# Query blocks aligned with key blocks, one tail block for two heads, and the decay bias added by VectorE's min-pass

## The chip, the core and the metric

The kernel runs on one core of a Trainium2 chip. The metric is device time in microseconds: median 670.79 us of three runs before the change (670.02 to 671.18). The core's engines are TensorE (PE in the profile; PEld is its weight load), VectorE (DVE), ScalarE (ACT), GpSimd (POOL) and SyncE (SP), which issues nearly all DMAs.

## The reference

Three blocks follow each other: causal attention with a cumulative decay bias, a gated spatial MLP with a layer norm and a residual, and a second one of the same kind without residual. B = 4, H = 8 heads, S = 576 positions, D = 64; model width 512, inner width 1024.

```python
scores = scale * q @ k.T                      # per batch and head, 576 x 576
cum = np.cumsum(np.maximum(s, 0.0), axis=-1)
bias = -(cum[:, :, :, None] - cum[:, :, None, :])
scores = np.where(causal, -1e9, scores + np.minimum(bias, 0.0))
attn = exp(scores - max) ; attn = attn / (sum + 1e-9)
x = (attn @ v) as [B, S, 512]
h = gelu(x @ w_in); u, v = halves of h; v = layer_norm(v) * g
x = x + (u * (w_sg @ v + b_sg)) @ w_out       # first MoE block
h = relu(x @ w_in2); ...                      # second, the same with its own weights
```

A row of the softmax does not change when a constant of the row is added, so only +cum of the key column has to be added to the scores.

## The kernel before

**Work and stages.** Two heads make a pair; 16 pairs run one after the other, four per batch. When the four pairs of a batch are done, its first MoE block can start, and is interleaved with the attention of the next batch; after the last pair come the rest of the first block and the second one. The float32 MoE products are made of three float32r matmuls each (high and low parts; lines 347 to 350, 425 to 427, 451 to 456, 471 to 473, 493 to 495).

**Order.** Every step (`plan.add`) has a place, a number on a time scale where a head is 1, and the steps it has to follow; `Plan.emit` takes the ready step of the lowest place. The tables `PAIR`, `HEAD`, `MOE`, `WEIGHT` and so on hold the places, `ENG` holds the engine (A, D, P) of each copy or small operation by phase. The scheduler of the tile framework then sets each engine's order.

**One pair.** `ldqk` loads queries and keys of both heads, `transposes` (T) turns them on PE with an identity (lines 621, 625), so that head 0 lies in partitions 0 to 63 and head 1 in 64 to 127. Query blocks are cut as 64, 128, 128, 128, 128 rows (`QB`), so that block i sees 64, 192, 320, 448 and 576 keys (`QN`). In `scores` each piece of a block (`PARTS`) is a float32 matmul per head over 64 partitions (line 660), and a second, float32r one (line 663) multiplies rows of ones by the rows of `bias` and adds the cumulative bias into the same PSUM bank. Line 668 is VectorE's min-pass: it adds the causal mask (bfloat16, `mask`), multiplies by -0.125, writes the result to SBUF and gives the row minimum; a second small instruction of that line reads the minimum out. Line 674 is ScalarE's exponential with the row sum.

`rows_of_bias` (K) loads four rows of 576 numbers, 9 KB, from `cum_d` into one of two `bias` buffers. `seg` transposes the weights in 15 blocks of 128 x 128 per head (line 737, `SEG`) and copies them from PSUM (`x0` to `x3`). `values` (V3) multiplies by the values in 12 matmuls per head (line 748, `USE`). `denominators` (R), `spread` (B) and `finish` (F1) divide: the sums are turned, written to `rec_d` in DRAM, read back broadcast, and multiplied in (line 754). All this draws on six PSUM banks (`psa`), the MoE on two (`psm`).

**Start.** `keep_busy` gives PE eleven dummy matmuls (line 145). `cumulate` makes the running sum `c8`, splits it in a high and a low part `ch`, and writes it to `cum_d`.

Of the kernel before, what the change touches and what calls it, by code (L numbers as in the profile page):

```python
# [9 lines left out]
F32 = mybir.dt.float32  # L10
# [20 lines left out]
PA, PM, XB, RAW, LOW, QKW = 6, 2, 3, 32, 0, 32  # L31

PAIR = {"ldqk": -7.15, "ldv": -7.77, "T": -0.93, "K": -10.12}
PAIR0 = {"ldqk": -3.69, "ldv": 1.93, "T": -27.82, "K": -1.85}
HEAD = {"S2": -3.76, "S4": -5.12, "R": -10.75, "B": -15.6, "X0": -0.48, "X1": 0.01, "X2": -6.24, "X3": 0.59,
        "V3": 0.77, "F1": -15.8}
HEAD0 = {"S2": -6.73, "S4": -4.13, "R": -2.05, "B": -8.21, "X0": -0.95, "X1": -7.32, "X2": -5.75, "X3": -0.43,
         "V3": -5.72, "F1": -7.2}

MOE = {"Va": (1.98, 2.55), "Vb": (-16.53, -3.57), "Vc": (-15.5, 25.31), "U": (3.84, 4.64), "ZY": (6.68, 5.45)}  # L40
WEIGHT = {"wv": (-0.99, 0.33), "wu": (6.32, 1.86), "sg": (2.65, 7.0), "wo": (-3.21, 6.28), "ahead": 3.45}
MOE2 = {"Va": (-18.47, 16.21), "Vb": (2.06, 8.91), "Vc": (-3.94, 3.37), "U": (4.67, 13.35), "ZY": (8.44, 23.03)}
WEIGHT2 = {"wv": (-0.12, 5.87), "wu": (10.83, 13.19), "sg": (10.11, 10.44), "wo": (3.64, 1.59), "ahead": 4.44}

MORE = {"t2": 15.57, "d2": 4.3, "sp": 3.41, "sp2": -1.39, "cut": 0.48, "xr": -24.01, "w0": 11, "cp": -3}


ENG = {"ra": "PPD.", "wlo": "DPPP", "wmin": "PPDP", "whi": "ADPD", "xhi": "PPAA", "xlo": "PDPP", "xdh": "...A",
       "xdl": "APAP", "vn": "...D", "vhi": "...A", "vlo": "...D", "ghi": "PDAP", "glo": "PDDP", "mu": "PDPP",
       "var": "PDPD", "rg": "...A", "tq": "AAD.", "tk": "DAA.", "tr": "DDD.", "vc": "PDD.", "vcl": "PPD.",  # L50
       "vdup": "PPP.", "x0": "DAD.", "x1": "ADD.", "x2": "AAA.", "x3": "DAD."}


def fl(ap):
    return ap.bitcast(F32)
# [35 lines left out]
def attention_two_moe_kernel(  # L91
# [65 lines left out]

    mask = const.tile([128, MW], BF16, name="mask")
    mask_f = mp.tile([128, 128], F32, tag="g", bufs=3, name="mask_f")
    nc.gpsimd.memset(mask, 0.0)  # L160
    nc.gpsimd.memset(mask_f, 0.0)
    nc.gpsimd.affine_select(out=mask_f, in_=mask_f, pattern=[[-1, 128]], compare_op=ALU.is_ge, fill=MASKED, base=0,
                            channel_multiplier=1)
    nc.gpsimd.tensor_copy(mask[:, MW - 128:], mask_f)
    cum_d = dr.tile([BH, 2, S], F32, name="cum_d")
# [383 lines left out]
    raw_v = [ap.tile([128, NB, 2, D], F32, name=f"raw_v{i}") for i in range(2)]  # L549
    for t in raw_v:  # L550
        nc.gpsimd.memset(t[64:128, NT], 0.0)
    pts, ptr = ([[place(f"{t}{j}_{i}", 128 * (i + 1), dt, pn * j + 64 * i * (i + 1)) for i in range(NB)] for j in range(3)]
                for t, dt in (("p", F32), ("r", F32R)))
    for p in pts:
        for i in range(NB):
            nc.gpsimd.memset(p[i][:, QN[i] if i else 0:], 0.0)
    raws = place("raw", rn, F32, 3 * pn), place("rawr", rn, F32R, 3 * pn)
    qk_d = [dr.tile([128, rn], F32, name=f"qk_d{n}") if 2 * n >= QKW else None for n in range(BH // 2)]
    mx = [ap.tile([128, NB], F32, name=f"mx{i}") for i in range(3)]
    sums = [ap.tile([128, 32], F32, name=f"sum{i}") for i in range(2)]  # L560
# [36 lines left out]
    def plan_pair(plan, n, st):  # L597
# [330 lines left out]
```

## Time and profile before

| | before |
|---|---|
| runs | 671.18, 670.79, 670.02 us (median 670.79) |
| span of the profiled execution | 667.5 us |
| PE busy | 645.1 us, 97% of the span |
| VectorE, ScalarE, GpSimd busy | 383.1, 327.6, 204.8 us |
| mean granted TensorE clock | 0.986 of full |

The span runs from the first to the last instruction of one profiled execution; the profile gives no separate time of that execution, so its span stands beside the runs' median, 3.3 us below it. Busy time is the union of an engine's instructions; matmul records overlap, so what a matmul costs is read from one start to the next.

### The profile page before, as it was taken

To read this page: it belongs to the slowest core of one execution; us is meant where nothing else is said; L and a number is where in the kernel's file an instruction comes from. 1 tells how busy PE (TensorE), PEld (TensorE's weight loads), DVE (VectorE), ACT (ScalarE), POOL (GpSimd) and SP (SyncE) were. 2 spreads that over 40 slices of the span, in tenths; PEclk is the share of its full clock that TensorE was granted. 3 is DMA by queue.
4 is the path that set the end of the run, shared out by engine and by line. 5 is a ranking of instruction groups with operands and counts; after the bars stand their busy time and mean duration, and the time that the engine had idled before them with its cause. 6 is when DMAs were issued, how large, how long until landed. Compare 5 with 4: busy or idle time off the path is not lost.

```text
span 667.5 us, 12894 instructions
## 1 busy us (share of the span) xinstructions
PE 645.1 (97%) x4733; PEld 564.8 (85%) x4733; DVE 383.1 (57%) x1109; ACT 327.6 (49%) x846; POOL 204.8 (31%) x332
## 2 busy tenths in 40 slices
PE   7988889999999999999999999999999999999997
PEld 4766767789988889988889999987998998998996
DVE  5898776565557787567784588557952322112110
ACT  3677668785135574435572356436532516414311
POOL 3232225531321100301110434544683246033032
PEclk8799899999999999999999999999999999999999
DMA  8378551232342312432312342364341000010011
GB/s 214 91 221 206 153 155 51 57 80 71 102 120 64 111 39 72 109 104 75 103 29 67 112 139 63 109 200 138 95 125 42 32 32 19 31 35 15 17 45 50
DMA packets 88024, 60.01 MB, mean 90 GB/s; under 512 B 65301, under 2 KB 73493, under 8 KB 87961
## 3 DMA queue, kind: packets, MB, share of 16 engines
q1 hardware_dynamic: 86760, 58.89, 31.5%
q8 instruction: 37, 0.61, 0.4%
q10 hardware_dynamic: 1200, 0.30, 0.2%
q14 instruction: 27, 0.21, 0.1%
HBM read 44.59 MB, written 14.57 MB: 89 GB/s over the span
## 4 chain that ended last, share of the span: by engine, by line
PE 81%; DVE 7%; DMA 6%; issue 2%; ACT 2%; SPq 1%; POOL 1%; DVEq 0%; POOLq 0%; ACTq 0%
PE pp L737 7%; PE s L660 7%; PE acc L748 6%; PE pm L347 3%; PE pm L425 3%; PE pm L348 3%; PE pm L427 3%; PE pm L426 2%; PE pm L451 2%; PE pb L453 2%; PE pb L452 2%; PE pb L451 2%; PE pm L453 2%; PE pm L452 2%; PE pb L427 2%
## 5 line engine op out<-in xcount | busy, mean ns | idle before, releaser
L674 ACT ACTIVATE p<-p,mx 128x576 f32<-128x576 f32 (+4 forms) x160 | 88.3, 553 | 31.8 <-DVE mx L668 31.2
L660 PE MATMUL s<-qk 64*128 64x288 f32 (+4 forms) x384 | 71.6, 427 | 3.7 <-ACT qk L179 1.3
L668 DVE CUSTOM_DVE_ANT_0 p<-s,mask 64x64 f32<-64x64 f32 (+4 forms) x160 | 61.5, 422 | 13.1 <-PE s L663 12.6
L737 PE MATMUL pp<-idf,p 128*128 128x128 f32 x480 | 64.5, 277 | 2.5 <-DVE mx L668 1.5
L737 PEld LDWEIGHTS pp<-idf,p 128*128 128x128 f32 x480 | 54.2, 141 | 7.1 <-issue 2.1
L457 DVE TENSOR_TENSOR u<-u,pb 128x320 f32<-128x320 f32 (+1 forms) x33 | 14.6, 454 | 73.2 <-PE pb L456 73.2
L663 PE MATMUL s<-bias,ones 64*128 64x288 f32 (+3 forms) x192 | 53.8, 488 | 0.0
L748 PE MATMUL acc<-pt,raw_v 128*64 128x64 f32 (+3 forms) x768 | 52.2, 287 | 0.2
L748 PEld LDWEIGHTS acc<-pt,raw_v 128*64 128x64 f32 x768 | 42.2, 140 | 11.1 <-issue 2.5
L301 POOL TENSOR_TENSOR xl<-x,xh 128x576 fp32r<-128x576 f32 x20 | 28.8, 1457 | 69.2 <-ACT xh L179 69.0
L179 POOL CAST g<-u 128x256 fp32r<-128x256 f32 (+1 forms) x40 | 17.2, 441 | 106.6 <-DVE u L457 77.8
L660 PEld LDWEIGHTS s<-qk 64*128 64x128 f32 (+1 forms) x384 | 34.7, 185 | 16.2 <-issue 5.8
L179 DVE COPY pt<-pp 128x512 f32<-128x512 f32 (+1 forms) x72 | 37.2, 530 | 12.4 <-PE pp L737 11.8
L179 ACT COPY pt<-pp 128x512 f32<-128x512 f32 (+2 forms) x56 | 28.7, 532 | 31.1 <-PE pp L737 31.1
L378 POOL TENSOR_TENSOR sm<-sm,half_pow 128x1 f32<-128x1 f32 (+1 forms) x38 | 25.7, 681 | 49.4 <-DVE sm L377 38.2
L452 PE MATMUL pb<-sgl,vh 128*128 128x320 f32 (+1 forms) x132 | 39.0, 296 | 0.0
L451 PE MATMUL pb<-sgh,vh 128*128 128x320 f32 (+1 forms) x132 | 38.9, 296 | 0.0
L451 PE MATMUL pm<-sgh,vh 128*128 128x256 f32 (+1 forms) x124 | 38.0, 307 | 0.7 <-DVE u L457 0.7
L452 PE MATMUL pm<-sgl,vh 128*128 128x256 f32 (+1 forms) x124 | 36.7, 296 | 0.0
L497 ACT COPY o<-pb 128x512 f32<-128x512 f32 x13 | 7.5, 589 | 57.1 <-PE pb L495 55.1
L425 PE MATMUL pm<-xh,inh 128*128 128x320 f32 (+1 forms) x112 | 35.4, 316 | 0.0
L374 POOL TENSOR_SCALAR sm<-sm 128x1 f32<-128x1 f32 (+1 forms) x33 | 7.9, 240 | 87.7 <-DVE g L297 73.5
(255 smaller groups left out, 1967.5 us busy)
## 6 DMA issues: line engine op xcount, KB each, us to landing
x<-rec_d SPq DMA_DIRECT2D x32, 144.0 KB
x_d<-x SPq DMA_DIRECT2D x16, 288.0 KB
x<-x_d SPq DMA_DIRECT2D x16, 288.0 KB
raw<-in_q_dram SPq DMA_DIRECT2D x32, 128.0 KB
stage<-in_moe_w_in_dram SPq DMA_DIRECT2D x8, 512.0 KB
raw_v<-in_v_dram SPq DMA_DIRECT2D x32, 128.0 KB
stage<-in_moe_w_in_dram SPq DMA_DIRECT2D x16, 256.0 KB
out_dram<-o SPq DMA_DIRECT2D x16, 256.0 KB
```

Source lines behind the costliest of these rows:

```text
L179: (e.copy if e is nc.scalar else e.tensor_copy)(out_, in_)
L301: engine("xlo", phase).tensor_tensor(xl[:, kk, :S], x, fl(xh[:, kk, :S]), ALU.subtract)
L425: nc.tensor.matmul(pu, W["inh"][:, kk, f], xh[:, kk, c], start=(kk == 0), stop=False)
L427: nc.tensor.matmul(pu, W["inl"][:, kk, f], xh[:, kk, c], start=False, stop=(kk == KD - 1))
L451: nc.tensor.matmul(pz, vh[sb][:, f], W["sgh"][:, sb, c], start=(sb == 0), stop=False)
L452: nc.tensor.matmul(pz, vh[sb][:, f], W["sgl"][:, sb, c], start=False, stop=False)
L660: nc.tensor.matmul(st[a, e][:m, c0:c0 + w], st["qk"][rows, 0, qc], st["qk"][rows, 1, kc], start=True, stop=False)
L663: nc.tensor.matmul(st[a, e][:m, c0:c0 + w], ones[rows, :m], bias[n % 2][rows, kc], start=False, stop=True)
L668: nc.vector.tensor_tensor_reduce(out=pts[g][i][:m, kc], in0=st[a, e][:m, c0:c0 + w], in1=mask[:m, d0:d0 + w], scale=-0.125, scalar=3e38 if ...
L674: nc.scalar.activation(p, p, AF.Exp, bias=mx[g][:m, i:i + 1], scale=-1.0, accum_out=sums[n % 2][:m, NB * e + i:NB * e + i + 1])
L737: nc.tensor.transpose(ps[:, w:w + 128].bitcast(like), pt[:, kb * 128:kb * 128 + 128], turned if qb == kb and kb else ident)
L748: nc.tensor.matmul(acc[a][D * e:D * e + D, a0:a0 + w], raw_v[m % 2][:, kb, e], pair["x", e, i][:, c0:c0 + w], start=j in (0, 1), stop=j in ...
```

## The change

- **Blocks.** Query blocks are rows 0 to 127, 128 to 255, 256 to 383 and 384 to 511, as the key blocks are; block i sees 128 (i + 1) keys. The last 64 queries of both heads become one block of 128 rows: `qtail` holds head 0's queries in partitions 0 to 63 and columns 0 to 63, head 1's in the other half, zeros elsewhere, and two matmuls of 288 key columns over all 128 partitions score both heads (`tail_scores`, S4).
- **Scores.** `bank` makes the other blocks: 512 columns, then 128 and 384 in one bank, then 256 (S2, S3). There is no bias matmul.
- **Bias.** `rows_of_bias` now loads the bias broadcast: `cb` holds it for 512 keys in all 128 partitions for both heads, `ct` holds head 0's 576 keys in partitions 0 to 63 and head 1's in the others; three DMAs. `masks` (M) lets GpSimd write the masked diagonal blocks beside them with five selects. The min-pass (`reduce`) takes the bias as its second input in place of the mask. Pair 0's bias is spread by four float32 matmuls (line 612, 614) from `c8` instead of DRAM. Pairs 1 and 3 use MoE buffers that are still free; from pair 4 on there is one tile `cb`, so that K of pair n follows S3 of pair n - 1.
- **Transposes and values.** Ten blocks per head and five for the tail (`tails`) instead of 15 per head; 7 value matmuls per head instead of 12, over the same 1600 columns per head. The transposed weights lie in two tiles per head.
- **Buffers.** Values and the tail's weights have one buffer (before, values had two).
- **Places and engines.** All tables of places have new numbers, and `ENG` moves some copies and MoE operations between ScalarE, VectorE and GpSimd. `keep_busy` has 12 matmuls instead of 11.

```diff
-PAIR = {"ldqk": -7.15, "ldv": -7.77, "T": -0.93, "K": -10.12}
+PAIR = {"ldqk": -4.84, "ldv": -15.84, "T": -0.93, "K": -8.08}
...
-        for e in range(2):
-            nc.sync.dma_start(out=fl(bias[0][D * e:D * e + D:32]), in_=fl(ch[e:e + 1]))
-        nc.sync.dma_start(out=cum_d, in_=fl(ch))
+        nc.sync.dma_start(out=cum_d, in_=c8)
...
+            copy("tr", phase, st["qk"][:, 1, cr], pr[:, 1])
+            for e in range(2):
+                rows = slice(D * e, D * e + D)
+                copy("ts", phase, qtail[rows, REM * e:REM * e + REM], pr[rows, 0])
...
+                for i in range(2):
+                    nc.tensor.matmul(ps[i], st0["sel"][:, i], st0["c8"][:, :512], start=True, stop=True)
+                for i in range(2):
+                    nc.tensor.matmul(ps[2 + i][:, :288], st0["sel"][:, 2], st0["c8"][:, 288 * i:288 * i + 288],
+                                     start=True, stop=True)
...
-                nc.sync.dma_start(out=fl(bias[n % 2][::32]), in_=cum_d[2 * n:2 * n + 2].rearrange("h i t -> (h i) t"))
+            rows = cum_d[2 * n:2 * n + 2]
+            nc.sync.dma_start(out=st["cb"][:, :, :512],
+                              in_=rows[:, :512].rearrange("(o h) t -> o h t", o=1).to_broadcast([128, 2, 512]))
+            for e in range(2):
+                nc.sync.dma_start(out=st["ct"][D * e:D * e + D], in_=rows[e:e + 1].to_broadcast([D, S]))
+
+        def masks():
+            cb, ct = st["cb"], st["ct"]
+            for e in range(2):
+                nc.gpsimd.affine_select(out=cb[:, e, 512:].rearrange("p (i c) -> p i c", i=NT - 1),
+                                        in_=cb[:, e, :384].rearrange("p (i c) -> p i c", i=NT - 1), pattern=[[0, NT - 1], [-1, 128]],
+                                        compare_op=ALU.is_ge, fill=MASKED, base=0, channel_multiplier=1)
...
-                for e in range(2):
-                    rows = slice(D * e, D * e + D)
-                    nc.tensor.matmul(st[a, e][:m, c0:c0 + w], ones[rows, :m], bias[n % 2][rows, kc], start=False, stop=True)
...
+        def reduce(out_, ps, bias, lowest, more):
+            nc.vector.tensor_tensor_reduce(out=out_, in0=ps, in1=bias, scale=-0.125,
+                                           scalar=lowest if more else 3e38, op0=ALU.add, op1=ALU.min, accum_out=lowest)
+
+        def bank(groups):
+            ps = [[psa.tile([128, 512], F32, tag="a", name="s") for e in range(2)] for _ in groups]
+            parts = [(j, c0, i, e) for j, group in enumerate(groups) for c0, i in group for e in range(2)]
+            for j, c0, i, e in parts:
+                rows = slice(D * e, D * e + D)
+                nc.tensor.matmul(ps[j][e][:, c0:c0 + 128 * i + 128], st["qk"][rows, 0, 128 * i:128 * i + 128],
+                                 st["qk"][rows, 1, :128 * i + 128], start=True, stop=True)
+            for j, c0, i, e in parts:
+                g, d, s_ = (2 * n + e) % 3, 512 + 128 * i, ps[j][e]
+                p, low, cb = pts[g][i], mx[g][:, i:i + 1], st["cb"][:, e]
+                if i == NT - 1:
+                    reduce(p, s_, cb[:, :512], low, False)
+                    continue
+                if i:
+                    reduce(p[:, :128 * i], s_[:, c0:c0 + 128 * i], cb[:, :128 * i], low, False)
+                reduce(p[:, 128 * i:], s_[:, c0 + 128 * i:c0 + 128 * i + 128], cb[:, d:d + 128], low, i)
...
+        def tail_scores():
+            ps = [psa.tile([128, 512], F32, tag="a", name="s") for i in range(2)]
+            low = ap.tile([128, 1], F32, tag="low", bufs=2, name="low")
+            for i in range(2):
+                c = slice(288 * i, 288 * i + 288)
+                nc.tensor.matmul(ps[i][:, :288], qtail, st["qk"][:, 1, c], start=True, stop=True)
+            for i in range(2):
+                c = slice(288 * i, 288 * i + 288)
+                reduce(ptail[:, c], ps[i][:, :288], st["ct"][:, c], low, i)
+            weights(NT, ptail, low)
...
+        plan.add(f"K{n}", t0 + where["K"], rows_of_bias, [f"S3.{n - 1 if n > 4 else n - 2}", f"K{n - 1}"])
+        plan.add(f"M{n}", t0 + where["K"] + MORE["mk"], masks, [f"K{n}"])
...
+    SEG = [[(0, 0), (1, 0), (1, 1)], [(2, 0), (2, 1), (2, 2)], [(3, 0), (3, 1), (3, 2), (3, 3)]]
+
+    USE = [(0, 0, 0, 256, 0, 0), (1, 0, 0, 320, 1, 0), (0, 0, 256, 128, 0, 128), (1, 1, 0, 320, 1, 0), (1, 2, 0, 320, 1, 0),
+           (1, 3, 128, 192, 1, 128), (0, 0, 384, 64, 1, 256)]
```

Three places show how the instructions move. At the start, PE has this order before (`pst` and `pr` are the transposes of pair 0's queries and keys, `s` its scores, `pp` transposed weights):

```order
L621 MATMUL pst<-idf,raw 128x128 x8
L625 MATMUL pr<-idf,raw 128x128
L660 MATMUL s_252<-qk 64x64
L660 MATMUL s_253<-qk 64x64
L660 MATMUL s_262<-qk 128x192
L660 MATMUL s_263<-qk 128x192
L660 MATMUL s_288<-qk 128x288
L660 MATMUL s_289<-qk 128x288
L663 MATMUL s_252<-bias_186,ones 64x64
L663 MATMUL s_262<-bias_186,ones 128x192
L663 MATMUL s_288<-bias_186,ones 128x288
```

and this one now:

```order
L612 MATMUL bc<-c_143,sel 128x512 x2
L614 MATMUL bc<-c_143,sel 128x288 x2
L595 MATMUL pst<-idf,raw 128x128 x8
L599 MATMUL pr<-idf,raw 128x128
L650 MATMUL s<-qk 128x512 x2
L650 MATMUL s<-qk 128x128 x2
L650 MATMUL s<-qk 128x384 x2
L650 MATMUL s<-qk 128x256 x2
L673 MATMUL s<-qk,qtail 128x288 x2
```

Four bias matmuls come first, and all score matmuls of pair 0 stand in ten rows; before, 24 score and bias matmuls did. In the mixed stage, PE's visit to a pair's scores begins like this before (`pm` is a MoE product):

```order
L427 MATMUL pm<-xh,inl 128x256
L660 MATMUL s_1811<-qk 64x64
L660 MATMUL s_1812<-qk 64x64
L663 MATMUL s_1811<-bias_187,ones 64x64
L663 MATMUL s_1812<-bias_187,ones 64x64
L660 MATMUL s_1821<-qk 128x192
L660 MATMUL s_1822<-qk 128x192
L663 MATMUL s_1821<-bias_187,ones 128x192
L663 MATMUL s_1822<-bias_187,ones 128x192
```

and now the four blocks of both heads, without the tail, stand together:

```order
L462 MATMUL pm<-g_1804,outh 128x256
L463 MATMUL pm<-g_1804,outl 128x256
L650 MATMUL s<-qk 128x512 x2
L650 MATMUL s<-qk 128x128 x2
L650 MATMUL s<-qk 128x384 x2
L650 MATMUL s<-qk 128x256 x2
L461 MATMUL pm<-g_1804,outh 128x256
```

No bias matmul is left between them, and over the whole order the stretches of score matmuls (with their bias matmuls) go from 32 to 22. SyncE issues one bias load of a pair before (`raw` are queries and keys, `rec_d` the denominators):

```order
L593 DMA raw<-in_k_dram 64x2x64
L326 DMA x_d_108<-x 128x576
L481 DMA xr<-x_d_107 128x320
L630 DMA bias_187<-cum_d 4x576
L684 DMA rec_d_182<-rt 4x32x32
```

and three now:

```order
L576 DMA raw<-in_k_dram 64x2x64
L622 DMA cb<-cum_d 128x2x512
L625 DMA cb<-cum_d 64x576 x2
L686 DMA rec_d_142<-rt 4x32x32
L692 DMA x<-rec_d_142 64x576 x2
```

The denominators of the pair before and their spread come behind them in the queue.

## Rows read from the trace of the kernel before

**Rows 1.** The page: busy time of each engine; granted clock in 40 slices.
```profile
PE 645.1 (97%) x4733; PEld 564.8 (85%) x4733; DVE 383.1 (57%) x1109; ACT 327.6 (49%) x846; POOL 204.8 (31%) x332
...
PEclk8799899999999999999999999999999999999999
```

**Rows 2.** Busy by stage: PE, PEld, DVE, ACT, POOL (xcount); PEclk; DMA; GB/s.
```profile
0.00:10.00 10.00, 6.05 (x20) 2.46 (x20) 6.41 (x16) 2.54 (x3) 4.86 (x31) 1.00 0.81 198
10.00:26.00 16.00, 15.96 (x71) 12.38 (x72) 9.69 (x35) 9.37 (x26) 3.34 (x5) 0.57 0.62 150
...
42.00:58.50 16.50, 14.74 (x135) 11.40 (x133) 16.26 (x52) 12.38 (x35) 6.43 (x8) 1.00 0.76 201
...
200.00:350.00 150.00, 150.00 (x1243) 130.07 (x1242) 108.83 (x346) 82.45 (x220) 18.94 (x28) 1.00 0.29 79
```

**Rows 3.** PE's timeline: start us, us, line, operation, out<-in, shapes.
```profile
209.22 0.33 PE L660 MATMUL s<-qk 64*64 64x64 f32 x4
...
210.79 0.50 PE L347 MATMUL pm<-inh,xh 128*128 128x512 f32 x1
...
213.72 1.02 PE L660 MATMUL s<-qk 64*128 64x448 f32 x4
...
214.78 0.70 PE L660 MATMUL s<-qk 64*128 64x320 f32 x4
...
215.47 0.65 PE L660 MATMUL s<-qk 64*128 64x288 f32 x4
...
216.17 0.42 PE L471 MATMUL pm<-g,outh 128*128 128x320 f32 x1
216.43 0.31 PE L472 MATMUL pm<-g,outh 128*128 128x320 f32 x1
216.58 0.31 PE L473 MATMUL pm<-g,outl 128*128 128x320 f32 x1
...
224.81 1.46 PE L748 MATMUL acc<-pt,raw_v 128*64 128x64 f32 x30
226.20 0.77 PE L737 MATMUL pp<-idf,p 128*128 128x128 f32 x5
...
228.56 2.12 PE L737 MATMUL pp<-idf,p 128*128 128x128 f32 x18
230.44 0.36 PE L425 MATMUL pm<-xh,inh 128*128 128x256 f32 x1
```

**Rows 4.** Score records of PE (L660) in 50 us of the mixed stage.
```profile
200.00:250.00 50.00, 7.67 (x48) 3.57 (x48) 1.00 0.27 73
```

**Rows 5.** Groups of VectorE, 0:100 us: shapes xcount | busy, mean ns | idle.
```profile
L206 DVE SCALAR_TENSOR_TENSOR stage<-stage 128x512 int32<-128x512 int32 x12 | 8.6, 714 | 0.1
...
L668 DVE CUSTOM_DVE_ANT_0 p<-s,mask 128x448 f32<-128x448 f32 x10 | 6.1, 616 | 1.0 <-PE s L663 0.8
...
L668 DVE DVE_READ_ACCUMULATOR2_ANT mx<- 128x1 f32 x50 | 4.0, 80 | 0.0
L668 DVE CUSTOM_DVE_ANT_0 p<-s,mask 128x192 f32<-128x192 f32 x10 | 3.3, 347 | 0.0
...
L179 DVE COPY qk<-pr 128x128 f32<-128x128 f32 x6 | 1.7, 279 | 0.0
```

**Rows 6.** PE's timeline at the start.
```profile
10.04 2.38 PE L660 MATMUL s<-qk 64*64 64x64 f32 x12 [0.77 <-DVE qk L179]
...
20.73 1.97 PE L621 MATMUL pst<-idf,raw 128*128 128x128 f32 x8
```

**Rows 7.** The chain that ended last, 0 to 110 us: start us, us, what.
```profile
38.00 5.08 DMA stage<-in_moe_w_in_dram
```

**Rows 8.** Groups of GpSimd, whole run: the 128-column select.
```profile
L162 POOL TENSOR_SCALAR_AFFINE_SELECT mask_f<-mask_f 128x128 f32<-128x128 f32 x1 | 0.3, 288 | 0.0
```

**Rows 9.** Timeline of all engines, 33 to 34 us.
```profile
33.11 0.62 POOL L204 TENSOR_SCALAR stage<-stage 128x512 f32<-128x512 f32 x1 [1.32 <-ACT stage L203]
...
33.21 1.06 DVE L206 SCALAR_TENSOR_TENSOR stage<-stage 128x512 int32<-128x512 int32 x1
```

More of the change, by code (lines that the diff above doesn't have):

```diff
@@ L41 @@
[L41 to L51, printed above, removed]
+PA, PM, XB = 6, 2, 3
@@ L156, in attention_two_moe_kernel @@
     g_b = const.tile([128, DF], F32, name="g_b")
[L158 to L165, printed above, removed]
+    cum_d = dr.tile([BH, S], F32, name="cum_d")
     sr = mp.tile([BH, S], F32, tag="vh", name="sr")
@@ L695, in plan_pair @@
-        plan.add(f"ldqk{n}", t0 + where["ldqk"], ldqk, [f"cp{n}", f"T{n - 1}"])
+        plan.add(f"ldqk{n}", t0 + where["ldqk"], ldqk, [f"T{n - 1}"])
         plan.add(f"ldv{n}", t0 + where["ldv"],
-                 lambda: load(raw_v[n % 2], v, b, j, raw_v[n % 2][0:REM, NT]), [f"V3.{n - 2}"])
-        plan.add(f"T{n}", t0 + where["T"], transposes, [f"ldqk{n}", f"S4.{n - 2}"])
-        plan.add(f"K{n}", t0 + where["K"], rows_of_bias, [f"S4.{n - 2}", f"K{n - 1}"])
-        plan.add(f"S2.{n}", t0 + head["S2"], lambda: [f(i) for i in range(NT) for f in (scores, move)],
-                 [f"T{n}", f"K{n}", f"S4.{n - 1}", f"X3.{2 * n - 2}", f"X3.{2 * n - 3}"])
@@ L740, in seg @@
-            st["x"][i] = pair["x", odd, i] = ap.tile([128, w], F32, tag=f"pt{odd}{i}", name="pt")
-            copy(f"x{i}", phase, st["x"][i], ps[:, :w])
+            p, x = pts[n % 3], pair["x"][odd]
+            for w, (qb, kb) in enumerate(SEG[i]):
+                nc.tensor.transpose(ps[:, w * 128:w * 128 + 128], p[qb][:, kb * 128:kb * 128 + 128], idf)
+            w = len(SEG[i])
+            if i:
+                copy(f"x{i}", phase, x[1][:, :w, 128 * i - 128:128 * i], ps[:, :w * 128].rearrange("p (k c) -> p k c", k=w))
+            else:
+                copy("x0", phase, x[0][:, :384], ps[:, :384])
@@ new lines, in tails @@
+        def tails():
+            ps = [psa.tile([128, 512], F32, tag="a", name="pp") for i in range(2)]
+            for w in range(NT):
+                nc.tensor.transpose(ps[0][:, w * 128:w * 128 + 128], ptail[:, w * 128:w * 128 + 128], idf)
+            nc.tensor.transpose(ps[1][:, :128], ptail[:, S - 128:], idf)
+            for e in range(2):
+                x = pair["x"][e]
+                copy("x3", 2 * e + min(phase, 1), x[1][:, :, 256:],
+                     ps[0].rearrange("p (k h c) -> p h k c", k=NT, h=2)[:, e])
+                copy("x4", 2 * e + min(phase, 1), x[0][:, 384:], ps[1][:, REM * e:REM * e + REM])
@@ L834, in attention_two_moe_kernel @@
     s14b = place("s14b", DF, F32R, pos + 8 * 128)
[L835 removed]
+    stg2 = w2p.tile([128, S + REM], F32, name="stg2")
+    rest["v"] = w2p.tile([128, DF], F32R, name="restv")
     nc.vector.tensor_scalar(s14b[64:128], g_b[64:128], 0.0, 1.0, ALU.mult, ALU.add)
```

203 lines of the change are left out of this document (86 added, 117 removed), and 4 rows, old and new, of the table SEG.

## The prediction

> **What bounds the kernel now.** I read four views, in this order. First the page's busy shares and its forty slices: TensorE is busy 97% of the span, and its granted clock is 90% or more of full in all slices but three of the first five [rows 1]. Then the busy time by stage, which splits the run in two. From 200 to 350 us, where attention and the first MoE layer are interleaved, PE is busy 150.00 of 150.00 us at full clock, VectorE only 108.83 and ScalarE 82.45: every PE microsecond saved there is a microsecond of the run. Before the first MoE matmul at 94.4 us it is otherwise. From 10 to 26 us PE is busy 15.96 of 16.00 us, at a granted clock of 0.57, and from 42 to 58.5 us it is VectorE that is full, 16.26 of 16.50 us [rows 2]. So the same saving counts in full in the mixed stage and hardly at all once VectorE sets the pace. Third, PE's timeline around one pair of heads in the mixed stage, which gives the price of each kind of matmul [rows 3]. Last, the groups by shape for VectorE, and single rows for the start, the DMA chain and GpSimd [rows 5 to 9].
>
> **Scores and bias.** A start here is compared with the next start on PE, because records overlap. One pair's scores and bias take 209.22 to 210.79 and 213.72 to 216.17, that is 1.57 + 2.45 = 4.02 us, in two visits [rows 3]. The 320-column piece runs from 214.78 to 215.47, 0.69 us for both heads: float32 scores (two records per matmul, the heads in the two halves of the rows) and one float32r bias matmul. A float32r matmul of 320 columns costs 0.15 us (216.43 to 216.58), which leaves 0.54 us for the scores, 1.69 ns per column [rows 3]. At 0.69 us per 320 columns, the pair's 1600 columns should take 3.45 us; the other 0.57 us goes to entering and leaving, 0.285 us per visit.
>
> The change drops the bias matmuls. Row blocks of 512, 384, 256 and 128 columns remain, 1280 x 1.69 = 2.16 us per pair. The tail of both heads becomes one full-height matmul of 2 x 288 columns. No row shows a float32 matmul of that form. If the halves now overlap perfectly, its price per column is the same, 2 x 288 x 1.69 = 0.97 us; if they run one after the other it would be half, 0.49 us; if filling the array doubled it, 1.95 us. I take 0.97, because the 320-column row fits halves that run together. The new order has 22 separate stretches of half-height matmuls where the old one had 32, 1.4 per pair, so 0.40 us of entering. New sum 2.16 + 0.97 + 0.40 = 3.53 us: **0.49 us saved per pair**, with ends 0.97 and -0.49.
>
> **Transposes and values.** Eighteen transposes run from 228.56 to 230.44 [rows 3], 0.104 us each. A pair needs 25 in place of 30: **0.52 us saved**. The value matmuls keep their 1600 columns per head but go from 24 to 14 per pair, 20 records fewer. The visit of 30 records from 224.81 to 226.20 [rows 3] gives 0.046 us per record, so 0.92 us is the most that could go if width did not matter; it does, and I take 0.
>
> Per pair that is 1.01 us. In steady flow a pair passes every 25 us (48 score records, two pairs of heads, in 50 us [rows 4]), and five of sixteen pairs are scored before the first MoE matmul. **Eleven pairs x 1.01 = 11.1 us** are saved where PE is full. What covers the rest is VectorE at 73% of that stage: two more min-passes per pair are added to it. By its shapes a pass costs 1.05 ns per column, from (616 - 347)/256, plus 145 ns and an 80 ns read [rows 5]. Columns fall from 3200 to 3136, so +0.45 - 0.07 = +0.38 us per pair. Replacing the bfloat16 mask with a float32 spread bias as second input is not shown; I take the same rate, at best nothing gained, at worst a pass that takes twice as long, 14 x 0.225 + 3136 x 0.00105 = 6.4 us more per pair, with which VectorE would just fill the 25 us period.
>
> **The first stage.** Pair 0's scores hold PE from 10.04 to 20.73 us, at the low clock [rows 2, 6]. At 1.2 GHz the new form needs about 2 x 3.53 = 7.1 us, 3.6 us less, and its five transposes fewer save 1.0 at that clock. Against that, spreading pair 0's bias by matmul adds 1600 full-height columns, 2.7 us at 2.4 GHz and 5.4 at 1.2, of which PE's 4 idle us in the first 10 [rows 2] can take most. Net some -3 us. What comes next is VectorE's full stretch, and there the change adds work: 0.38 us per pair for passes and about 0.35 for two 64-column copies (half the width of the 279 ns copy [rows 5], less one narrower copy), 5 x 0.4 = 2 us after the narrower copies of transposed blocks are set off. Net -1 us, between -7 (the low clock, 0.43 of 16 us, is avoided altogether) and +8 (below).
>
> **Loads and masks.** Per pair SyncE now issues three bias loads, some 800 KB, where it issued one of 9 KB, and GpSimd five mask selects. A 512 KB weight load stood 5.08 us on the chain [rows 7], so 800 KB take 5 to 8 us. A 128-column select takes 0.288 us [rows 8]; the 384-column ones lie between that and three times it, nearest to the 0.62 us of a 512-column GpSimd pass [rows 9], say 1.9 us per pair (1.45 to 2.9). From pair 5 on the bias tile is single: load and mask stand between the last min-pass of one pair and the first of the next. About half of the 25 us period lies between them, less 4 us of passes still queued, so 8 us against 5 + 1.9. I take it as just hidden, cost 0. Values and the tail tile lose their second buffer too; they are read once per pair, and the next load has most of a period. After the last pair nothing of weight changes; I set new places of MoE steps at 0, +-2 us.
>
> **Sum.** The profiled span is 667.5 us; the median is 670.8 us, so 3.3 us lie around it, taken as fixed. 667.5 - 11.1 - 1 = 655.4, and with 3.3 the time is **658.7 us**. By its bounds it runs from 647 (11 pairs at 1.01 + 0.48 us, and the low clock gone: -23) to 668 (the +8 of the first stage; the tail at double price gives the same).
>
> **Rivals.**
> - *The late bias tile (slower).* Where load and masks take 11 us (8 + 2.9) instead of the 8 that are free, VectorE, which works in order, stands 3 us in each of 11 pairs, and the MoE passes queued behind it hold PE. 33 us lost, 11 gained: 691 us; half of it, if PE has half of the time other work, 675. It decides from 9 us on, where 11 pairs x 1.1 us eat the gain. For it: the load is ten times what it was, and SyncE's queue has other waits ahead of it. Against: DMA engines are busy only 0.29 in that stage [rows 2].
> - *The load on the first stage.* DMA is at 0.62 to 0.81 there [rows 2]; four bias loads join in. If one of them stands on the chain, +8 us: 667.
> - *Masks against VectorE.* A two-input pass took 1.06 us at 33.21 where its group's mean is 0.71, while GpSimd worked from 33.11 to 33.73 [rows 5, 9]. If half of the 25 early selects hold such a pass for 0.4 us, +5 us: 664. The Trainium skill, SBUF — State Buffer, "Who interferes with whom", states that a VectorE instruction with two SBUF inputs and a GpSimd instruction that reads SBUF exclude each other for a whole instruction. By that rule the min-passes, with one input in PSUM, are spared, and this row agrees.
> - *No low clock.* PE gets work from 6 to 10 us and stays at 2.4 GHz: 6 us more than forecast, 652.
> - *It doesn't save what it says.* The tail at 1.95 us per pair costs 11 x 0.97 = 10.7 us and gives back the gain: 669.
>
> **Chances.** Forecast (653 to 663) 0.60; no low clock 0.13; first-stage load or masks 0.12; late bias tile 0.10; tail at double price 0.05. The measurement tells 0.2% (1.3 us) from no change. Faster: 0.60 + 0.13 + 0.11 = 0.84; same 0.04; slower 0.12. The range 647 to 668 leaves out the late tile and the edges.
>
> **What would show it.** In the changed profile PE should stay at 150 of 150 us in the mixed stage, a pair's scores should take 3.5 us and not 4, and transposes 0.104 us each with 400 in place of 480 (320 + 80). The 320- and 512-column groups should show 1.69 ns per column for both heads together, and the tail 0.49 us per matmul. I am wrong if VectorE's min-passes wait for GpSimd or for the bias load in the mixed stage, if PE has gaps there, or if the first MoE matmul comes later than 94.4 us.

## The result, and the profile after

| | before | after |
|---|---|---|
| runs beside each other | 670.98 us median (670.02 to 672.25, 4 runs) | 649.59 us (647.77 to 652.21, 4 runs) |
| ratio, 95% interval | | 0.9693 [0.9658, 0.9727] |
| profiled execution: span, own time | 667.5 us | 650.4 us, 652.21 us |
| PE busy | 645.1 us | 627.0 us |

The change saves 21 us, 3.1%. The forecast was 12 us and 658.7; the measured time lies in its range of 647 to 668, but outside the 653 to 663 that it thought likeliest. The direction and the main term were right. The rest below asks where the other 9 us came from.

The page of the changed kernel (busy time of each engine; granted clock in 40 slices) answers to [rows 1]:

```profile
PE 627.0 (96%) x4086; PEld 536.2 (82%) x4086; DVE 406.3 (62%) x1258; ACT 332.1 (51%) x861; POOL 217.1 (33%) x327
...
PEclk9789997999999999999999999999999999999999
```

PE lost 18 us of busy time, VectorE gained 23. The busy time by stage (as [rows 2], with one stage more at 68 us), first of the changed kernel, then that stage of the kernel before:

```profile
10.00:26.00 16.00, 11.28 (x61) 8.49 (x60) 14.51 (x51) 10.05 (x27) 9.55 (x16) 0.79 0.98 243
42.00:58.50 16.50, 11.80 (x73) 8.32 (x75) 16.36 (x54) 10.85 (x30) 4.24 (x6) 0.79 0.72 190
68.00:94.40 26.40, 24.00 (x163) 17.69 (x160) 23.43 (x72) 16.57 (x47) 14.83 (x19) 1.00 0.80 195
200.00:350.00 150.00, 150.00 (x1085) 128.50 (x1086) 113.28 (x404) 82.10 (x225) 36.87 (x59) 1.00 0.40 114
```

```profile
68.00:94.40 26.40, 22.68 (x221) 18.52 (x219) 19.13 (x59) 17.61 (x50) 7.13 (x12) 0.94 0.58 165
```

From 200 to 350 us nothing has changed in kind: PE 150.00 of 150.00, VectorE 113.28. So the mixed stage is still PE's, as forecast. From 10 to 68 us VectorE is now nearly full (14.51 of 16 us from 10 to 26, where it was 9.69). The last rows of both are what the prediction had not looked at: from 68 us to the first MoE matmul of the kernel before, VectorE was busy only 19.13 of 26.40 us.

PE's timeline around two pairs of heads in the mixed stage of the changed kernel (start us, us, line, operation, out<-in, shapes) answers to [rows 3]:

```profile
309.88 1.13 PE L673 MATMUL s<-qk,qtail 128*128 128x288 f32 x4
310.85 1.04 PE L595 MATMUL pst<-idf,raw 128*128 128x128 f32 x8
311.72 0.27 PE L599 MATMUL pr<-idf,raw 128*128 128x128 f32 x1
...
315.56 2.43 PE L650 MATMUL s<-qk 64*128 64x512 f32 x16
317.92 0.39 PE L415 MATMUL pm<-xh,inh 128*128 128x256 f32 x1
```

The tail takes 309.88 to 310.85, **0.97 us**, the price that was chosen between 0.49 and 1.95. All four row blocks of both heads, in one visit, take 315.56 to 317.92 (2.36 us; the MoE matmul behind them starts there). The sum is 3.33, where 4.02 stood and 3.53 was forecast. Some pairs are scored in two visits of one head each, 1.92 + 1.49 us, so the mean over eleven pairs is higher: 3.7 (from all visits of these pairs, start to next start, in a second profile of the same kernel; 4.14 before). The eight transposes from 310.85 to 311.72 cost 0.109 us each; a pair has five fewer.

VectorE's groups by shape from 200 to 350 us (shapes xcount | busy us, mean ns | idle) show the min-pass with the spread bias:

```profile
L642 DVE CUSTOM_DVE_ANT_0 p<-s,cb 128x512 f32<-128x512 f32 x12 | 8.0, 685 | 1.2 <-PE s L650 1.1
...
L642 DVE CUSTOM_DVE_ANT_0 ptail<-s,cb 128x288 f32<-128x288 f32 x6 | 2.7, 450 | 0.0
```

685 ns for 512 columns is what the old pass would take (145 + 1.05 x 512 = 683), and 450 ns for 288 columns stand where the old pass took 445 in the same stretch: float32 and bfloat16 second inputs cost the same, as assumed. From 100 to 350 us one min-pass waits for GpSimd's masks, and none for the bias load (VectorE's waits: engine, output, line, what it waited for: us, times, longest):

```profile
DVE ptail L642 <- POOL cb L638: 1.1, 1, 1.1
```

Last, PE's timeline at the end of the first stage, before (with one row of the busy time by stage, whose 0.51 is the granted clock) and after:

```profile
67.40 0.66 PE L220 MATMUL pm<-idf,stage 128*128 128x128 f32 x4 [2.27 <-DMA stage<-in_moe_w_sg_dram]
...
68.10 4.64 PE L748 MATMUL acc<-pt,raw_v 128*64 128x320 f32 x48
...
68.00:70.00 2.00, 2.00 (x13) 1.14 (x13) 0.96 (x2) 1.97 (x7) 0.18 (x2) 0.51 0.36 66
...
94.37 0.47 PE L347 MATMUL pm<-inh,xh 128*128 128x512 f32 x1
```

```profile
61.55 0.66 PE L210 MATMUL pm<-idf,stage 128*128 128x128 f32 x4 [0.56 <-DMA stage<-in_moe_w_sg_dram]
...
80.95 0.50 PE L337 MATMUL pm<-inh,xh 128*128 128x512 f32 x1
```

In the kernel before, PE stood 2.27 us until 67.40 for a weight load, and its clock then fell (0.51 from 68 to 70 us). In the changed kernel the same matmuls wait 0.56 us, until 61.55, and the first MoE matmul comes at 80.95 instead of 94.37 us. It is tempting to take the wait and the clock for the cause, but two other profiles speak against it. The first two rows are the changed kernel again (run c0_after), the last two run f3_late below, whose pairs 0 to 4 and whose order are those of the kernel before:

```profile
64.26 0.65 PE L210 MATMUL pm<-idf,stage 128*128 128x128 f32 x4 [1.91 <-DMA stage<-in_moe_w_sg_dram]
...
83.19 0.50 PE L337 MATMUL pm<-inh,xh 128*128 128x512 f32 x1
```

```profile
68.00:94.40 26.40, 22.27 (x225) 18.27 (x226) 22.01 (x68) 19.70 (x55) 9.07 (x12) 0.99 0.61 173
...
93.86 0.66 PE L347 MATMUL pm<-inh,xh 128*128 128x512 f32 x1
```

With a wait of 1.91 us the changed kernel still starts its MoE at 83.19 us; with the clock at 0.99 from 68 to 94.4 us the old order still starts it at 93.86.

**An account.** I cut both profiles at 95 us, where both have scored pairs 0 to 4 in full. For each group of matmuls I add the time from each start to the next one, without idle gaps, times the granted clock. "Again" is the profile of run c0_after below, the same kernel.

| after 95 us | before | after | again | change |
|---|---|---|---|---|
| scores, bias, tail | 45.4 | 39.2 | 39.9 | -6.2, -5.5 |
| transposes | 44.1 | 37.3 | 38.8 | -6.8, -5.3 |
| values | 36.8 | 37.4 | 37.6 | +0.6, +0.8 |
| MoE | 435.1 | 427.8 | 428.3 | -7.3, -6.8 |
| PE idle | 3.6 | 1.5 | 2.8 | -2.1, -0.8 |
| lost to the low clock | 0.0 | 5.1 | 0.0 | +5.1, 0.0 |

Scores, transposes and values together give 12.4 and 10.0 us. But by 95 us the changed kernel has also scored pair 5's tail (0.97 us, at 89.67 and 92.13) and done eight query and key transposes (0.87 us) more than the old one, which is work moved forward and not work saved. Without it, and with six transposes of pair 4 that the second profile does only behind the cut, 10.6 and 8.8 us were saved (11.1 forecast). Of MoE's 7, 4.8 us had been done before the cut (5.6 against 0.8 us). So 6.6 us of later work lie ahead of 95 us: the early start. The other 2 to 2.5 us of MoE lie at the edge of the +-2 given for the new places; that the places made them cheaper is not shown.

Up to 95 us PE did about as much work in all: 72.4 us before (71.8 in f3_late), 72.9 and 71.0 after. Pairs 0 to 4 needed 6 to 7 us less of it, the four matmuls that spread the bias included; idle time rose from 13.1 to 16.2 and 17.6 us, and the low clock took 4.7 and 6.5 us instead of 8.5.

### The profile page after: what moved, and what is told of

The parts are those of the page before. It is cut to its first block, busy times and chain, and to the rows that moved or that the text cites. A ratio compares the mean times of both kernels' runs of the same rounds, so it can differ in the third digit from the quotient of the medians.

```text
span 650.4 us, 11947 instructions
## 1 busy us (share of the span) xinstructions
PE 627.0 (96%) x4086; PEld 536.2 (82%) x4086; DVE 406.3 (62%) x1258; ACT 332.1 (51%) x861; POOL 217.1 (33%) x327
## 4 chain that ended last, share of the span: by engine, by line
PE 78%; DVE 9%; DMA 7%; ACT 2%; issue 2%; POOL 1%; SPq 0%; ACTq 0%; DVEq 0%; POOLq 0%
PE acc L755 7%; PE s L650 5%; PE pp L726 5%; PE pm L337 3%; PE pm L338 3%; PE pm L415 3%; PE pm L340 3%; PE pm L416 2%; PE pm L417 2%; PE s L673 2%; PE pm L441 2%; PE pst L595 2%; PE pm L442 2%; PE pm L443 2%; PE pb L441 2%; PE pb L443 2%
## 5 line engine op out<-in xcount | busy, mean ns | idle before, releaser
L666 ACT ACTIVATE p<-p,mx 128x128 f32<-128x128 f32 (+3 forms) x128 | 70.8, 556 | 15.8 <-DVE mx L642 14.9
L169 ACT COPY pt<-pp 128x384 f32<-128x384 f32 (+2 forms) x92 | 41.6, 486 | 32.8 <-PE pp L726 30.2
L452 POOL TENSOR_TENSOR g<-u,g 128x256 fp32r<-128x256 f32 (+1 forms) x32 | 25.7, 808 | 93.0 <-ACT g L169 93.0
L169 ACT CAST g<-u 128x256 fp32r<-128x256 f32 (+1 forms) x48 | 20.5, 433 | 63.9 <-DVE u L447 61.0
L755 PE MATMUL acc<-pt,raw_v 128*64 128x320 f32 (+4 forms) x448 | 52.9, 373 | 0.1
L642 DVE CUSTOM_DVE_ANT_0 p<-s,cb 128x128 f32<-128x128 f32 (+2 forms) x128 | 48.3, 416 | 2.9 <-PE s L650 2.6
L650 PE MATMUL s<-qk 64*128 64x384 f32 (+3 forms) x256 | 47.3, 467 | 0.8 <-DVE qk L169 0.8
L631 POOL TENSOR_SCALAR_AFFINE_SELECT cb<-cb 128x384 f32<-128x384 f32 x32 | 17.1, 555 | 89.2 <-DMA cb<-cum_d 61.2
L726 PE MATMUL pp<-idf,p 128*128 128x128 f32 x320 | 45.4, 281 | 1.2 <-DVE x L761 1.2
L650 PEld LDWEIGHTS s<-qk 64*128 64x128 f32 x256 | 26.5, 194 | 15.4 <-issue 7.1
L415 PE MATMUL pm<-xh,inh 128*128 128x256 f32 (+1 forms) x112 | 35.1, 313 | 0.0
L337 PE MATMUL pm<-inh,xh 128*128 128x512 f32 x84 | 34.5, 410 | 0.6 <-DVE xh L169 0.6
```

Of the source, the lines that this page charges most:

```text
L169: (e.copy if e is nc.scalar else e.tensor_copy)(out_, in_)
L337: nc.tensor.matmul(ps, xh[:, kk, c], hi, start=(kk == 0), stop=False)
L415: nc.tensor.matmul(pu, W["inh"][:, kk, f], xh[:, kk, c], start=(kk == 0), stop=False)
L642: nc.vector.tensor_tensor_reduce(out=out_, in0=ps, in1=bias, scale=-0.125, scalar=lowest if more else 3e38, op0=ALU.add, op1=ALU.min, accu ...
L650: nc.tensor.matmul(ps[j][e][:, c0:c0 + 128 * i + 128], st["qk"][rows, 0, 128 * i:128 * i + 128], st["qk"][rows, 1, :128 * i + 128], start= ...
L666: nc.scalar.activation(p, p, AF.Exp, bias=low, scale=-1.0, accum_out=sums[n % 2][:, c:c + 1])
```

## Experiments

Twelve kernels. "Before" in each is the median beside it. Those named e and q let the scheduler order the instructions anew, which turned out to be a change of its own; the four named f hold the order of every engine. No run holds the order alone, without an edit.

**c0_after**: the changed kernel again. 

> The changed kernel again, unedited, beside the others of this group: 649.6 us as before, between 647 and 653. The span of each run says what lies outside it: 1.8 us if the four runs so far are typical, not the 3.3 that the prediction took.

Measured 651.44 us (649.08 to 652.52, before 669.76), ratio 0.9718 [0.9694, 0.9742]. In every run of both kernels the time is 1.7 to 1.9 us above the span. The 3.3 us of the prediction were these 1.8 and the difference between one execution and the median of others. Over both groups the gain is 18 to 21 us.

**e2_mixed, e1_early**: work added to PE (e1_early with `n < 5` as its condition).

```diff
-                nc.tensor.matmul(ps[j][e][:, c0:c0 + 128 * i + 128], ...)
+                for _ in range(2 if i >= 2 and 6 <= n < 11 else 1):
+                    nc.tensor.matmul(ps[j][e][:, c0:c0 + 128 * i + 128], ...)
```

> The same doubling in pairs 6 to 10 in place of pairs 0 to 4: the same 7.6 us of TensorE work, now where PE is busy 150 of 150 us. Theory of the prediction: +7.6 us (within 1.5). Rival (VectorE or the bias load sets the pace of a pair there): +0 to +3.

> The changed kernel, in which pairs 0 to 4 issue the score matmuls of their 384- and 512-column blocks twice (the second overwrites the first with the same numbers): 896 columns of both heads at 1.69 ns, 1.5 us of TensorE work per pair, 7.6 us in all, before the first MoE layer has really begun. Theory A, as the prediction had it (VectorE sets the pace until the first MoE matmul): the added work is hidden, 0 to +1 us. Theory B (TensorE sets the end there too, because VectorE is full only up to about 60 us): +2 to +4, the work of pairs 3 and 4. Theory C (every TensorE microsecond counts everywhere): +7.6.

Measured: e2_mixed 668.78 us, +17.3 on c0_after; e1_early 677.98, +26.5. Both above every theory, and the traces say why. In e2_mixed PE's work (as in the account, whole run) is 633.5 us against 618.2, +15.3, twice the estimate. In several of these pairs the two copies of one head now stand together. From e2_mixed's PE timeline:

```profile
225.09 1.98 PE L651 MATMUL s<-qk 64*128 64x512 f32 x4
227.00 0.39 PE L415 MATMUL pm<-xh,inh 128*128 128x256 f32 x1
```

Four records of one head take 1.91 us, 0.95 per block with entering and leaving (they start 0.43 us apart), while two heads in turn take 0.86 for the same block (run f1_early, below). One head alone costs as much as both. (The Trainium skill, TensorEngine Tiling (Array Packing), "Key Properties", lets tiles of the array work in parallel; here they do where the two heads' matmuls alternate.) So the 15.3 us of work cost 17.3 us of time, though in a new order (2.1 us more idle time, 1.9 less of low clock): in the mixed stage PE's work counts in full, as forecast. In e1_early the work grew by 13.4 and the idle time by 9.1 us. Its order differs in thousands of rows, and it decides nothing.

**q2_places**: the kernel before with the new places of the MoE steps and weights alone. 

> The kernel before, with nothing but the changed kernel's places of the MoE steps and weights (the tables MOE, WEIGHT, MOE2, WEIGHT2 and five entries of MORE). The prediction set the new places at 0, +-2 us: 669 to 673. Rival (the first MoE matmul at 81.0 us in place of 94.4 comes from the places): 661 to 666, with the first MoE matmul before 90 us.

Measured 681.36 us (before 669.76), 1.7% slower, first MoE matmul at 95.32 us. Alone in the old kernel the new places cost 11.6 us. Both theories fell, and how much of the 21 us they are worth in the new one can't be told by this.

**q3_nobias**: the kernel before without its bias matmuls. 

> The kernel before without its 192 float32r bias matmuls, all else kept (the decay bias is left out of the scores). By the prediction's row price, 1600 columns per pair at 0.15 us per 320, 0.75 us per pair: -8.3 us over eleven pairs, up to -12 if the early pairs count too. Rival (the bias matmuls cost what lies between their starts and the next starts in the trace, 12.6 us for six pairs in 200 to 350 us): -23 us and more. What the aligned blocks and the tail add or take is then the rest up to the changed kernel's -21.

Measured 667.88 us (before 669.72), ratio 0.9971 [0.9953, 0.9989]. PE's work fell from 636.5 to 625.3 us, 0.70 per pair, as the row price said; but its idle time rose from 16.7 to 23.7 us and the low clock took 11.5 us instead of 8.5. The work went, and the new order gave most of it back, as the next two runs bear out.

**f3_late, f3_early**: the same, with the order held. Each engine's instructions are chained in the order of the kernel before, and only the bias matmuls of some pairs go (their score matmuls then end the accumulation themselves). The cut shows f3_late; f3_early has `n < 5` in place of `n >= 5`.

```diff
-                    nc.tensor.matmul(st[a, e][:m, c0:c0 + w], ..., start=True, stop=False)
-                for e in range(2):
+                    nc.tensor.matmul(st[a, e][:m, c0:c0 + w], ..., start=True, stop=n >= 5)
...
+                for e in range(0 if n >= 5 else 2):
                     ...
                     nc.tensor.matmul(st[a, e][:m, c0:c0 + w], ones[rows, :m], bias[n % 2][rows, kc], start=False, stop=True)
```

> The kernel before without the bias matmuls of pairs 5 to 15 (their decay bias is left out of the scores), and with every engine's instructions held in the order that they had in the kernel before, so that nothing but these 132 matmuls goes. The first try without them let the scheduler find a new order: TensorE's work fell by 11.2 us (0.70 per pair), but its idle time rose by 7. If TensorE's work alone sets the end of the mixed stage and the order is what gave it back, eleven pairs at 0.70 to 0.75 us are seen in full: -7 to -9 us. Rival (another engine sets the pace when TensorE gets faster): 0 to -4.

> The same with the bias matmuls of pairs 0 to 4 left out in place of those of pairs 5 to 15, the order held again: 60 matmuls, 3.5 to 3.8 us of TensorE work at full clock (a little more where the clock is low). Theory A, as the prediction had it (VectorE sets the pace until the first MoE matmul, so this is hidden): 0 to -1 us. Theory B (VectorE sets it to about 60 us only, and then TensorE): -1 to -2.5. Theory C (it counts in full): -3.5 to -5.

Measured: f3_late 662.25 us (before 669.24), ratio 0.9905 [0.9868, 0.9942], -7.0 us. The visits of a pair's scores show where:

```profile
306.45 1.34 PE L660 MATMUL s<-qk 64*64 64x64 f32 x12
307.72 0.50 PE L347 MATMUL pm<-inh,xh 128*128 128x512 f32 x1
...
310.66 2.05 PE L660 MATMUL s<-qk 64*128 64x448 f32 x12
312.64 0.41 PE L471 MATMUL pm<-g,outh 128*128 128x320 f32 x1
```

1.27 and 1.98 us stand for 1.57 and 2.45 in [rows 3], 0.77 less; the mean over the eleven pairs is 4.14 to 3.42, 8 us in all. The time fell by 7.0 (interval 3.9 to 8.8). In the profile the time behind 95 us fell by 6.9: 8.5 us less of score work by the account, 1.1 us lost to the low clock and 0.7 more for values. So within the interval this saving counts in full in the mixed stage; the rival's 0 to 4 just touches it.

f3_early: 663.86 us, ratio 0.9919 [0.9891, 0.9947], -5.4 us (interval 3.5 to 7.3). Theory C by its size, but not by its place. VectorE's first min-pass, before and then here:

```profile
12.65 0.22 DVE L668 CUSTOM_DVE_ANT_0 p<-s,mask 64x64 f32<-64x64 f32 x1 [2.56 <-PE s L663]
```

```profile
9.81 0.22 DVE L670 CUSTOM_DVE_ANT_0 p<-s,mask 64x64 f32<-64x64 f32 x1 [0.56 <-PE s L660]
```

It comes 2.8 us earlier. The ends of the last min-pass of each pair, in us, one profile each (f3_late has pairs 0 to 4 as before, c0_after is the changed kernel again, so these two rows show the scatter):

| pair | 0 | 1 | 2 | 3 | 4 |
|---|---|---|---|---|---|
| before | 21.4 | 35.9 | 52.2 | 68.0 | 86.7 |
| f3_late | 21.0 | 36.7 | 52.9 | 69.8 | 85.8 |
| f3_early | 18.1 | 30.9 | 48.3 | 64.0 | 82.7 |
| after | 20.9 | 35.4 | 51.6 | 67.7 | 82.7 |
| c0_after | 21.5 | 36.4 | 53.3 | 69.9 | 85.2 |

The gain of f3_early is made at pairs 0 and 1, where in the kernel before PE runs at the low clock (0.57 from 10 to 26 us) and VectorE is busy 9.69 of 16 us. What pairs 2 to 4 save adds nothing: against "before" the lead stays at 4 us. By 95 us f3_early has done 5.2 us of MoE work, where the kernel before has done 0.8. The changed kernel, which spreads pair 0's bias first, has no such lead at pairs 0 to 3. Its 4.0 us at pair 4 stand in one profile; between c0_after and f3_late they are 0.6.

**f1_early**: PE work added to pairs 0 to 4 of the changed kernel, order held, heads in turn.

```diff
+                if n < 5 and i >= 2 and e == 1:
+                    for f in range(2):
+                        rows = slice(D * f, D * f + D)
+                        EXTRA.append(nc.tensor.matmul(
+                            ps[j][f][:, c0:c0 + 128 * i + 128], st["qk"][rows, 0, 128 * i:128 * i + 128],
+                            st["qk"][rows, 1, :128 * i + 128], start=True, stop=True).ins.name)
```

(`EXTRA` tells the held order which matmuls are new.)

> The changed kernel with the score matmuls of the 384- and 512-column blocks of pairs 0 to 4 issued twice, the two heads in turn so that their halves run together, and every engine's order held as in the changed kernel: 1.5 us of TensorE work per pair, 7.6 us in all. In the changed kernel VectorE is busy 23.4 of 26.4 us from 68 to 94.4 us, more than in the kernel before (19.1). Theory A (hidden by VectorE until the first MoE matmul): 0 to +2. Theory C (counts in full): +7 to +9. Between them: what counts is the part behind the score matmuls that VectorE waits for.

Measured 652.18 us (before 669.24), ratio 0.975 [0.9716, 0.9785], against 0.9718 of c0_after: +0.3%, 2 us, with intervals that overlap (the widest difference they allow is 6 us, below theory C's 7 to 9). The work is there and the start of the MoE lies between those of the two profiles without it (80.95 and 83.19 us):

```profile
11.54 1.05 PE L655 MATMUL s<-qk 64*128 64x512 f32 x4
12.40 1.06 PE L650 MATMUL s<-qk 64*128 64x128 f32 x8
...
81.16 0.50 PE L337 MATMUL pm<-inh,xh 128*128 128x512 f32 x1
```

The doubled 512-column blocks take 11.54 to 12.40 us, 0.86. PE's idle time is 15.7 us, where it was 17.7 and 20.4. In the changed kernel the early stage hides most of 7.6 us of added PE work (theory A). That VectorE sets its pace there is the likeliest reading (23.43 of 26.40 us busy), but no run made VectorE faster.

**e5_dma0**: pair 0's bias loaded instead of spread by matmuls (`if n == 0` made false). 

> The changed kernel with pair 0's bias loaded from DRAM like the others, without the four matmuls that spread it. If VectorE sets the pace of the first stage, its first min-pass (12.8 us) comes later by the write of the sums, the load of 800 KB and the masks, some 4 to 8 us, and most of it counts: +3 to +7 us. Rival (TensorE's 3.2 us at the start are what counts): -2 to 0.

Measured 676.31 us (before 669.72), +25 on c0_after. The first min-pass comes at 19.14 us, waiting for the load, against 13.7 in c0_after. That lies within the 4 to 8 us expected for it; the time missed the +3 to +7, and the order is another one, which starts the MoE at 125 us. The first part is shown, the size of its effect is not.

**e3_load, e4_mask**: the bias load, and the masks, three times from pair 5 on (`for _ in range(3 if n > 4 else 1)` around them). 

> The changed kernel with each bias load from pair 5 on issued three times, 2.4 MB in place of 0.8 MB per pair. In the changed kernel the masks of pairs 5 to 15 end 0.7 to 12.5 us before the next min-pass. If the single bias tile is just hidden, as forecast, 6 to 10 us more of load exceed that in most pairs: VectorE waits 2 to 8 us per pair, and about half of it reaches PE: +15 to +40 us. Rival (hidden with much room): 0 to +3.

> The changed kernel with the five mask selects of pairs 5 to 15 done three times: 1.9 us of GpSimd become 5.8, no DMA added. By the room read in the trace (0.7 to 12.5 us, under 3.9 in five of eleven pairs) VectorE waits some 9 us in all, and PE half of it at most: 0 to +5 us. If GpSimd's selects hold VectorE's passes as well (the shared port), the min-passes that lie beside them get longer by up to 4 us per pair: +10 us and more, and the group's mean of the 512-column min-pass rises above 0.70 us.

Measured: e3_load 698.49 us, +47 on c0_after, more than the +15 to +40 expected; its order is a new one. VectorE's waits from 100 to 350 us (columns as above):

```profile
DVE ptail L643 <- DMA cb<-cum_d: 34.3, 7, 6.9
```

There the slower rival happens: the first pass of a pair waits for its bias. In the changed kernel it is hidden. Its SyncE, GpSimd and VectorE around one pair:

```profile
321.04 0.37 SPq L622 DMA_DIRECT2D cb<-cum_d  x1
...
326.64 0.53 POOL L638 TENSOR_SCALAR_AFFINE_SELECT cb<-cb 64x64 f32<-64x64 f32 x2
...
330.08 0.45 DVE L642 CUSTOM_DVE_ANT_0 ptail<-s,cb 128x288 f32<-128x288 f32 x1
```

The load is issued at 321.04 us, the two last masks start at 326.64 and take 0.53, so all is there 6.1 us after the issue and 2.9 before the next min-pass. "Just hidden" was right (8 us free and 6.9 needed were forecast), and the room is small. e4_mask: 664.71 us, +13 where 0 to +5 was expected; VectorE's waits for masks are 5.6 us in five pairs, and order and masks can't be told apart. But its 512-column min-pass answers the question of the port:

```profile
L643 DVE CUSTOM_DVE_ANT_0 p<-s,cb 128x512 f32<-128x512 f32 x20 | 13.4, 687 | 0.7 <-PE s L651 0.6
```

687 ns beside three times the GpSimd selects, 685 without. The Trainium skill, SBUF — State Buffer, "Who interferes with whom", spares a pass with one input in PSUM, and this agrees.

**f4_warm**: dummy matmuls in two gaps of PE, order held (the first 32 here, 24 more behind pair 1's tail transposes).

```diff
+            if n == 0:
+                for _ in range(32):
+                    EXTRA.append(nc.tensor.matmul(ps[1][:, 384:384 + 128], qtail, idf, start=True, stop=True).ins.name)
```

> The changed kernel, order held, with dummy matmuls (idf by qtail, into unused columns) in two gaps of TensorE: 32 behind pair 0's tail scores, 24 behind pair 1's tail transposes, so that the granted clock does not fall behind these gaps (each low stretch of some 7 us loses 2.5 to 3.5 us of TensorE's work). If TensorE sets the end there, -3 to -6 us. If VectorE does, 0 to -2. If the clock falls all the same elsewhere: 0.

Measured 667.36 us, +16. It failed as a test. The dummies share a tile with the tail scores and so wait for VectorE's min-pass on it:

```profile
20.93 10.17 PE L680 MATMUL s<-idf,qtail 128*128 128x128 f32 x64 [3.31 <-DVE low L642]
30.93 1.04 PE L595 MATMUL pst<-idf,raw 128*128 128x128 f32 x8
```

They run from 20.93 to 30.93 us, pair 1's transposes start at 30.93 in place of 19.43, and the first MoE matmul comes at 98.72 us. It shows only that a delay of pair 1, 11.5 us here, reaches the start of the MoE and the end; the 24 later dummies add to it. What the low clock costs stays open.

## Why the prediction was right, and where it was off

The measured 649.6 us lie outside the 653 to 663 that got 0.60. By number they are nearest to the rival "no low clock" (652), which did not happen. So the main term was right by its mechanism, and that the time fell in the range owes something to the range's width.

- **Scores, 0.49 us per pair**: 0.41 to 0.48 by the account, pair 5's tail included. Nearly right, the tail's 0.97 to the digit. f3_late shows the price of the bias matmuls by itself, 0.77 in the pair shown.
- **Transposes 0.52, values 0**: 0.52 and 0.45 in the two profiles (five fewer per pair, at 0.105 and 0.107 us each, 0.104 before); values +0.06. Right.
- **Eleven pairs in full**: right. PE 150 of 150 us; added work costs its own time (e2_mixed), removed work gives it (f3_late).
- **The first stage, -1 us**: mis-sized, and this is the main miss. Its parts were off both ways: "net some -3 us" at pair 0 did not come (21.4 became 20.9 and 21.5), and pair 3 ends at 67.7 and 69.9 instead of 68.0 and, in f3_late, 69.8. The step that failed is "What comes next is VectorE's full stretch": the window from 42 to 58.5 us was taken for all that lies before the first MoE matmul, and what PE saves there was put at nothing. From 68 to 94.4 us VectorE was busy 72% of the time (83% in f3_late), and by 95 us 6.6 us of later work (4.8 of MoE, 1.8 of attention) were done. The 6 to 7 us that PE no longer spends on pairs 0 to 4 are of that size, and f3_early too moved 4.4 us of MoE ahead by removing PE work there. On the other side f1_early adds such work almost without cost. What lets the saved work through stays open: neither the weight load's wait nor the clock at 68 us explains it, by the two profiles above, and the new order, which puts 16 MoE matmuls among pair 3's value matmuls, was not tried by itself in the changed kernel.
- **Places, 0 +- 2**: MoE matmuls 2 to 2.5 us cheaper, idle time after 95 us 1 to 2 less. At the edge, if the places are their cause.
- **3.3 us outside the span**: 1.8. This did not move the forecast, which is the median of 670.8 less 12.1; the other 1.5 is the profiled execution's distance from that median.
- **Where the 9 us lie.** Five are in the profiles: the span fell by 17.1 and 16.8 us instead of 12.1. The early start gave 6.6 in place of 1, MoE and idle time 4.6 and 2.8 in place of 0, attention 0.5 and 2.3 less than forecast, and one of the two profiles lost 5.1 us to the low clock. The other four are scatter: the profiled execution was 1.5 us below its median before (667.5 + 1.8 against 670.8) and 2.6 above it after (652.2 against 649.6).

Rivals: the late bias tile did not happen, but e3_load shows that it is real, once 1.6 MB more are loaded per pair. An early bias load did stand on the chain that ended last in the changed kernel (start, us, what):

```profile
52.97 6.11 DMA cb<-cum_d
```

In c0_after it was 7.29 us, from 54.95. The forecast time of that rival, 667 us, did not come with it: pair 3 ended at 67.7 and 69.9 us, against 68.0 and 69.8 with the old loads. "Masks against VectorE" meant VectorE's early passes with two inputs, and these did get longer, the 12 of this group from 714 [rows 5] to 889 ns on average:

```profile
L196 DVE SCALAR_TENSOR_TENSOR stage<-stage 128x512 int32<-128x512 int32 x12 | 10.7, 889 | 0.1
```

With the 12 of the line before it (726 to 837 ns) that is 3.4 us of VectorE. But of the eight that took over 0.8 us only two lay beside a mask select; the others lay beside other GpSimd passes. The low clock did not vanish: 4.7 and 6.5 us lost before 95 us, against 8.5. The doubled price of the tail was wrong; by the prediction's own terms it would have made 669, not the 668 of its upper bound.

## What to carry to other kernels

Split the run by what is full in each window, and cover it without gaps: a stage that was not looked at holds the error. When a scheduler orders the instructions, hold the order before reading an edit's price: dropping the same kind of matmul was worth 2 us in all pairs with a free order, 7.0 in eleven of them with a fixed one. Work saved on the full engine counted nearly one for one (7.0 of 8 us). For a stage where two engines are nearly full, ask with an edit in each direction: here added work was hidden (f1_early, in the changed kernel), while removed work was not (f3_early, in the old one).

## What was not expected of the hardware

- A head's half-height float32 matmul alone takes as long (0.95 us for 512 columns, entering and leaving included) as those of two heads in the two halves of the rows together (0.86).
- The granted clock fell to 0.50 from 96 to 106 us while PE was busy 10.00 of 10.00 us, behind a gap of 1.24 us. It did so in one profile of this kernel and not in the other, and cost 5 us. The first four executions took 652.2, 650.3, 648.9 and 647.8 us at mean clocks of 0.980, 0.984, 0.989 and 0.992; but the six of c0_after do not go with the clock (652.5 us at 0.989, 649.1 at 0.987), so the clock alone does not make the scatter. The gap, from PE's timeline, and the busy time by stage:

```profile
93.84 0.30 PE L599 MATMUL pr<-idf,raw 128*128 128x128 f32 x1 [1.24 <-issue]
...
96.00:106.00 10.00, 10.00 (x35) 5.27 (x36) 9.81 (x39) 8.63 (x22) 1.72 (x5) 0.50 0.13 29
```
